# Up and down products as whole phases of 16 steps, attention half a period later, DMA transposes from unit 8 on

## The chip, the cores and the metric

The kernel runs on one core of one Trainium2 chip. The metric is the device time of the whole program in microseconds, lower is better. Most executions agree within about 0.3%. Twice in this study an execution ran far slower (519 us and 794 us); those are marked slow and no comparison uses them. Ratios are computed as the mean time of one kernel's fast runs over the mean of the other's fast runs of the same rounds, so they are not quite the ratio of the medians quoted beside them.

In this kernel PE does all matrix products, and its weight loads (PEld) run beside them; PE writes into banks of a memory called PSUM, from which ACT and DVE read. ACT does the gelu and copies finished rows out of PSUM, DVE does masks and scalings, POOL scales v and issues most loads, and SP issues DMA transposes and stores. The granted clock of a trace is the share of PE's full rate that the profile reports.

## The reference, cut to what matters

```python
# q, k, v: (8, 8, 576, 64) f32;  w_in: (512, 2048);  w_out: (2048, 512)
scores = q @ k.T / 8                        # per batch and head
ret    = scores * gamma_h ** (i - j) * (i >= j)
x      = (ret @ v) -> rows of (4608, 512)   # heads side by side
h      = x @ w_in
out    = (h * sigmoid(1.702 * h)) @ w_out
```

It is a decaying linear attention (a retention layer) followed by a two-layer network. The attention has little arithmetic; the two matrix products after it have most of it.

## The kernel before: the parts that matter

The 4608 rows are 36 units of 128 rows. Four units make a chunk of 512 rows, nine chunks in all. For each chunk, `up` is 16 steps of 4 matmuls (hidden block f, then gelu on ACT), `down` is 16 steps of 4 matmuls (row block r = i // 4). Each step is 4 matmuls of 512 columns.

```python
def up(c, f):
    bank = f"H{count['up'] % 2}"            # two PSUM banks, in turn
    ...                                     # 4 matmuls into bank
    op("act", ... gT[c % 2][:, f, :] <- gelu(bank))

def down(c, i, ybanks):
    r, s = divmod(i, 4)
    bank = ybanks[r % len(ybanks)]
    ...                                     # 4 matmuls; with s == 3 the bank is full:
    op("act", ... osb[u % 4] <- bank)       # four buffers for output rows
    op("sp",  ... out <- osb[u % 4])        # store, in SP's queue

def transpose_dma(u):                       # SP's queue too, waits for k and q of u
    op("sp", lambda e: e.dma_start_transpose(qkT[u % NQT].ap(), kq[sl]...), ...)

def block(m):                               # attention of units a = 2m, b = 2m + 1
    inter(a); inter(b)                      # state part, banks O0, O1
    scores(a + 2); scores(b + 2)            # of the next pair, banks S0/S1 and S2/S3
    scores_out(a + 2, 0)                    # DVE: mask, PSUM -> SBUF
    values(a); values(b)                    # PE, into O0, O1
    values_out(a); values_out(b)            # DVE: O0, O1 -> xT, the input of `up`
    ...                                     # DVE: rest of the masks
    if m > 4:
        ready_t(m + 3); fetch(m + 4, 2 * m + 6); ready_v(m + 2)
```

Every program order is fixed by hand: each engine has one in-order stream, and a small helper finds the semaphore waits. `fetch` issues loads on POOL's queue; its loads of v are made to wait until a given DMA transpose has landed.

The order of the products before, cut:

```python
play(16, lambda f: up(0, f), {...})                # chunk 0 up, units 4 to 6 between
...
play(8, lambda i: up_half(1, i, 1), {              # chunk 1 up, in two halves
    2: [lambda: head_in(8, "dve", "S2")],          # units 8, 9 transposed on PE
    4: [lambda: head_in(9, "dve", "S0")],
    6: [lambda: ready_v(4), lambda: scores_of(4)]})
play(16, lambda i: down(0, i, ("H0", "H1")), {..., 6: [lambda: block(4)], ...})
for m in range(5, NU // 2 + 1):                    # then half periods: downs of chunk c - 1
    ...                                            # alternate with ups of chunk c
    for x in "DDDDBDDUDDUUUUUUU" if m == 5 else "DDUDUDUDUDUDDUUU":
        ...                                        # D: down, banks S2 and S0;  U: up;  B: block
```

## Time and profile before

| | before |
|---|---|
| device time, median | 309.64 us (309.44 to 310.19, 6 runs) |
| span of the profiled run | 308.4 us |
| PE busy | 297.2 us (96%) |
| ACT, DVE, POOL busy | 121.3, 134.8, 113.0 us |
| PE idle between 60 and 80 us | 1.6 us |

Two rows of the profile page of the kernel before: part 1 gives busy time, share and instructions; in part 2 each digit is the busy share, in tenths, of one of 40 slices of the span.

```profile
PE 297.2 (96%) x2133; PEld 156.7 (51%) x2168; DVE 134.8 (44%) x279; ACT 121.3 (39%) x214; POOL 113.0 (37%) x139
PE   7799999999899999999999999999999999999996
```

PE is busy nearly throughout; the dips are the start, the end and the slice from 77 to 85 us. The view by windows, 60 to 80 us (window, length, busy time of PE, PEld, DVE, ACT and POOL, granted clock, DMA share, GB/s), has the 1.6 us of idle PE:

```profile
60.00:80.00 20.00, 18.40 (x155) 9.64 (x157) 11.31 (x22) 2.77 (x5) 9.91 (x12) 1.00 1.02 168
```

The Trainium skill ("Trainium Kernel Development and Optimization", section Performance Expectations) warns that matmul busy time is a bad measure of distance to the limit. The better reading here is the time from one matmul's start to the next, taken from the trace's records: 216 ns for 512 columns, 56 ns for 128. The kernel has 2168 matmuls (as many as the weight loads counted), the trace has 2133 records of them, so 35 are missing; a gap of exactly one more slot is a missing record and not a stall.

The timeline of PE in the kernel before (start, length, engine, line, operation, count) shows the first ten ups of chunk 0, one after the other:

```profile
19.38 8.81 PE L455 MATMUL psH<-xT,w_in_sb 128*128 128x512 bf16 x40
```

The next group starts at 28.02, so 40 matmuls took 8.64 us: 216 ns each, with gelu keeping up. The same timeline with all engines, between 58 and 79 us, holds the two places where PE waits for more than 0.5 us after the start (bracket: idle time before, and what ended it; SPq is SP's queue, and its length runs over merged issues, waits between them included):

```profile
58.74 15.87 SPq L339 DMA_TRANSPOSE qkT<-kq  x4
62.50 0.40 PE L415 MATMUL psS<-qkT 64*128 64x128 bf16 x8
63.39 0.40 PE L415 MATMUL psS<-qkT 64*128 64x128 bf16 x8 [0.49 <-DMA qkT<-kq]
...
74.67 1.54 SPq L500 DMA_DIRECT2D out_dram<-osb  x3
76.64 0.40 PE L415 MATMUL psS<-qkT 64*128 64x128 bf16 x8
77.12 0.60 ACT L494 ACTIVATE osb<-psS 128x512 f32<-128x512 f32 x1 [3.68 <-PE psS L415]
77.77 0.40 PE L415 MATMUL psS<-qkT 64*128 64x128 bf16 x8 [0.73 <-ACT osb L494]
```

At 63 us the scores of unit 11 wait for its DMA transpose. At 77 us the scores of unit 13 wait for ACT to empty the bank that the down product has just filled. By start-to-start times these two cost 0.68 and 0.92 us.

Two pieces of the chain of waits (start, length, what) say why the transpose at 63 us was late:

```profile
44.88 13.78 DMA kq<-in_q_dram
58.74 3.30 DMA qkT<-kq
```

A load of 128 KB took 13.8 us to land, in a backlog of weights and of v 8 to 11; its transpose then took 3.3 us.

### The profile page before, as it was taken

To read this page: it belongs to the slowest core of one execution; us is meant where nothing else is said; L and a number is where in the kernel's file an instruction comes from. 1 tells how busy PE (TensorE), PEld (TensorE's weight loads), DVE (VectorE), ACT (ScalarE), POOL (GpSimd) and SP (SyncE) were. 2 spreads that over 40 slices of the span, in tenths; PEclk is the share of its full clock that TensorE was granted. 3 is DMA by queue.
4 is the path that set the end of the run, shared out by engine and by line. 5 is a ranking of instruction groups with operands and counts; after the bars stand their busy time and mean duration, and the time that the engine had idled before them with its cause. 6 is when DMAs were issued, how large, how long until landed. Compare 5 with 4: busy or idle time off the path is not lost.

```text
span 308.4 us, 5131 instructions
## 1 busy us (share of the span) xinstructions
PE 297.2 (96%) x2133; PEld 156.7 (51%) x2168; DVE 134.8 (44%) x279; ACT 121.3 (39%) x214; POOL 113.0 (37%) x139
## 2 busy tenths in 40 slices
PE   7799999999899999999999999999999999999996
PEld 3444688544454545454545454545445454544444
DVE  5782863773764543545364725271717250100000
ACT  8566345211343333333333333334343424344411
POOL 9799991062462633614635606071000000000000
PEclk9999999999999999999999999999999999999999
DMA  9999999999999979999899999999610101010122
GB/s 141 194 207 189 189 205 184 138 132 165 175 215 125 166 164 153 192 177 144 202 144 194 159 124 155 134 143 123 61 66 5 52 19 36 34 60 31 45 53 85
DMA packets 116007, 39.93 MB, mean 129 GB/s; under 512 B 104912, under 2 KB 109264, under 8 KB 115984
## 3 DMA queue, kind: packets, MB, share of 16 engines
q0 software_dynamic: 80016, 22.55, 68.7%
q1 hardware_dynamic: 35968, 17.05, 23.8%
q8 instruction: 17, 0.28, 0.4%
q14 instruction: 6, 0.05, 0.0%
HBM read 36.70 MB, written 9.44 MB: 150 GB/s over the span
## 4 chain that ended last, share of the span: by engine, by line
PE 73%; POOL 13%; DMA 11%; issue 2%; SPq 0%; ACT 0%; DVE 0%; POOLq 0%; ACTq 0%
PE psS L486 32%; PE psH L455 31%; POOL kq L203 6%; DMA kq<-in_q_dram 6%; POOL vn L217 3%; PE psO L434 2%; DMA vn<-in_v_dram 2%; PE psS L415 2%; POOL vp L303 2%; PE psS L348 2%; PE psO L396 1%; PE psO L486 1%; DMA qkT<-kq 1%; POOL w_out_sb L232 1%; DMA out_dram<-osb 1%
## 5 line engine op out<-in xcount | busy, mean ns | idle before, releaser
L455 PE MATMUL psH<-xT,w_in_sb 128*128 128x512 bf16 x489 | 123.5, 379 | 2.4 <-issue 1.7
L460 ACT ACTIVATE gT<-psH 128x512 bf16<-128x512 f32 x128 | 76.4, 597 | 115.4 <-PE psH L455 115.4
L486 PE MATMUL psS<-w_out_sb,gT 128*128 128x512 bf16 x472 | 115.9, 379 | 0.5 <-issue 0.2
L455 PEld LDWEIGHTS psH<-xT,w_in_sb 128*128 128x128 bf16 x512 | 47.8, 98 | 58.4 <-ACT gT L460 3.5
L486 PEld LDWEIGHTS psS<-w_out_sb,gT 128*128 128x128 bf16 x480 | 46.1, 98 | 52.0
L217 POOL DMA_DIRECT2D vn<-in_v_dram x39 | 33.7, 882 | 93.3 <-DMA qkT<-kq 77.9
L424 DVE TENSOR_TENSOR pm<-psS,mask 128x512 bf16<-128x512 f32 x64 | 41.3, 683 | 41.1 <-PE psS L415 41.0
L203 POOL DMA_DIRECT2D kq<-in_q_dram x39 | 34.9, 904 | 0.0
L203 POOL DMA_DIRECT2D kq<-in_k_dram x39 | 34.8, 899 | 0.0
L494 ACT ACTIVATE osb<-psS 128x512 f32<-128x512 f32 x30 | 17.9, 597 | 32.9 <-PE psS L486 29.2
L444 DVE TENSOR_TENSOR xT<-psO,gq 128x512 bf16<-128x512 f32 x36 | 23.4, 684 | 13.9 <-PE psO L434 13.3
L378 DVE TENSOR_TENSOR kvf<-psS,kvf 64x256 f32<-64x256 f32 x24 | 10.1, 422 | 25.1 <-PE psS L348 24.8
L303 DVE TENSOR_TENSOR vp<-vn,vfac 128x512 bf16<-128x512 f32 x29 | 18.8, 684 | 1.4 <-DMA vn<-in_v_dram 1.3
L518 DVE COPY osb<-psS 128x256 f32<-128x256 f32 x1 | 0.4, 425 | 41.4 <-PE psS L512 41.4
L472 PE MATMUL psH<-xT,w_in_sb 128*128 128x256 bf16 x128 | 15.2, 273 | 0.0
L486 PE MATMUL psH<-w_out_sb,gT 128*128 128x512 bf16 x62 | 14.2, 379 | 0.2 <-issue 0.2
L415 PE MATMUL psS<-qkT 64*128 64x128 bf16 x288 | 12.3, 218 | 2.1 <-ACT qkT L331 0.9
L381 DVE CAST kv<-kvf 64x256 bf16<-64x256 f32 x36 | 13.3, 369 | 1.2
L477 ACT ACTIVATE gT<-psH 128x512 bf16<-128x512 f32 x16 | 9.6, 597 | 10.7 <-PE psH L472 10.7
L472 PEld LDWEIGHTS psH<-xT,w_in_sb 128*128 128x128 bf16 x128 | 12.0, 98 | 1.8 <-issue 0.2
L348 PEld LDWEIGHTS psS<-vp,kq 128*128 128x128 bf16 x128 | 9.2, 98 | 7.0 <-ACT kv L361 0.7
L348 PE MATMUL psS<-vp,kq 128*128 128x128 bf16 x128 | 12.4, 219 | 0.2 <-POOL vp L303 0.2
(62 smaller groups left out, 152.8 us busy)
## 6 DMA issues: line engine op xcount, KB each, us to landing
vn<-in_v_dram POOLq DMA_DIRECT2D x31, 256.0 KB, 5.0
out_dram<-osb SPq DMA_DIRECT2D x31, 256.0 KB, 2.4
kq<-in_k_dram POOLq DMA_DIRECT2D x31, 128.0 KB, 5.7
kq<-in_q_dram POOLq DMA_DIRECT2D x31, 128.0 KB, 5.8
w_in_sb<-in_moe_w_in_dram POOLq DMA_DIRECT2D x4, 512.0 KB, 10.0
w_out_sb<-in_moe_w_out_dram POOLq DMA_DIRECT2D x4, 512.0 KB, 14.4
out_dram<-osb SPq DMA_DIRECT2D x10, 128.0 KB, 2.3
vn<-in_v_dram POOLq DMA_DIRECT2D x8, 128.0 KB, 4.3
```

What stands on the lines that cost most here:

```text
L203: e.dma_start(kq[sl][p0 : p0 + n, i, :].rearrange("p (h d) -> p h d", d=DH), src[b, :, s0 : s0 + n, :].rearrange("h p d -> p h d"),)
L217: e.dma_start(vn[sl][p0 : p0 + n, :, :], v[b, :, s0 : s0 + n, :].rearrange("h p d -> p h d"),)
L303: op(eng, lambda e: e.tensor_tensor(vp[u % NVP].ap(), vn[sl].ap(), vfac[:, ty, :, None].to_broadcast([P, H, DH]), ALU.mult), reads=[f"vn{s ...
L348: op("pe", lambda e, hp=hp: e.matmul(kb[:, hp, :], kq[sl][:, 0, P * hp : P * hp + P], vp[u % NVP][:, 2 * hp : 2 * hp + 2, :], start=(first ...
L415: op("pe", lambda e, hp=hp, hh=hh, bank=bank: e.matmul(by_pair(bank)[:, hp, :], qt[64 * hh : 64 * hh + 64, hp, :], qt[64 * hh : 64 * hh + ...
L424: op("dve", lambda e: e.tensor_tensor(pm[u % 4][hh].ap(), by_pair(bank), m[:, None, :].to_broadcast([P, HP, P]), ALU.mult), reads=[bank, " ...
L444: op("dve", lambda e: e.tensor_tensor(xT[ch % 3][:, :, 128 * j : 128 * j + 128], by_pair(bank), gq[:, ty, :, :], ALU.mult), reads=[bank] + ...
L455: op("pe", lambda e, a=a: e.matmul(hb, w_in_sb[:, a, P * f : P * f + P], xT[c % 3][:, a, :], start=(a == 0), stop=(a == HP - 1)), reads=[f ...
L460: op("act", lambda e: e.activation(gT[c % 2][:, f, :], hb, AF.Gelu_apprx_sigmoid), reads=[bank], writes=[f"gT{c % 2}_{f}"])
L472: op("pe", lambda e, a=a, f=f, j=j: e.matmul(hb[:, j, :], w_in_sb[:, a, P * f : P * f + P], xT[c % 3][:, a, n], start=(a == 0), stop=(a == ...
L486: op("pe", lambda e, f=f: e.matmul(y, gT[c % 2][:, f, P * r : P * r + P], w_out_sb[:, f, :], start=(f == 0), stop=(f == NF - 1)), reads=[f ...
L494: op("act", lambda e: e.activation(osb[o].ap(), y, AF.Copy), reads=[bank], writes=[f"osb{o}"])
```

## The change

It aims at runs of one kind of product (16 ups, then 16 downs), with a paired attention block near the end of each run, and at having no PE transposes after unit 7. With ups and downs apart, both use banks H0/H1, and S0 to S3 belong to attention alone. The attention of a pair comes half a period later than before, so its transposes have longer. The diff, cut to its core:

```diff
         def head_vs(u):                     # values beside the next unit's scores
+            inter(u)
+            values(u)
+            values_out(u)
+            if u < 7:
+                head_s(u + 1)
             head_k(u, "dve")
 ...
-            if m > 4:
-                ready_t(m + 3)
-                fetch(m + 4, 2 * m + 6)
-                ready_v(m + 2)
+            if m + 2 < NU // 2:
+                ready_t(m + 2)
+                fetch((2 * m + 6, 2 * m + 7), (2 * m + 6, 2 * m + 7), 2 * m + 4)
 ...
+        scale_v(3, "pool")
         load_win(3)
-        scale_v(3, "pool")
 ...
-        for u in range(8, 12):
-            load_v(u)
-        load_kq(10)
-        load_kq(11)
 ...
+        ready_t(4)                          # units 8, 9 by DMA
+        fetch((8, 9), (10, 11), 8)          # these loads wait for the transpose of 8
 ...
-        play(8, lambda i: up_half(1, i, 1), {
-            2: [lambda: head_in(8, "dve", "S2")],
-            4: [lambda: head_in(9, "dve", "S0")],
-            6: [lambda: ready_v(4), lambda: scores_of(4)],
-        })
-        play(16, lambda i: down(0, i, ("H0", "H1")), {... 6: [lambda: block(4)], ...})
-        for m in range(5, NU // 2 + 1): ...  # "DDUDUDUDUDUDDUUU"
+        play(8, lambda i: up_half(1, i, 1), {})
+        steps = [(down, 0), (down, 1)]
+        for c in range(2, NCH):
+            steps += [(up, c), (down, c)]
+        events = {
+            (0, 2): [lambda: scores_of(4)],
+            (0, 5): [lambda: ready_t(5), lambda: fetch((10, 11, 12, 13), (12, 13), 10)],
+            (0, 7): [lambda: ready_v(4)],
+            (0, 9): [lambda: state(9)],
+        }
+        for m in range(4, NU // 2):
+            p = m - 4
+            events[p, 15 if m == 4 else 13] = [lambda m=m: block(m)]
+            ...                              # states at steps 4, 7; v scaled at 9
+        for p, (step, c) in enumerate(steps[:-1]):
+            ...                              # 16 steps of `step`, each followed by its events
```

`events[p, i]` runs after step i of phase p.

More of the change, by code (lines that the diff above doesn't have):

```diff
@@ L366, in state @@
         def state(u, bank="S1"):
+            if u >= NU or unit_info(u)[1] == 2:
+                return
             pb, kind, c = unit_info(u)
-            if kind == 2:
-                return
             kb = state_mm(u, bank, True)
@@ L553, in head_k, with head_vs, fetch @@
                 state(u, "S3")
-        def head_mid(u):
-            head_s(u)
-        def head_out(u):
-            head_v(u)
+        def head_vs(u):
+            inter(u)
[3 more added lines that the diff above has]
+                head_s(u + 1)
             head_k(u, "dve")
-        def fetch(m, held=None):
-            after = () if held is None else [f"qkT{held % NQT}q"]
-            for u in (2 * m, 2 * m + 1):
+        def fetch(vs, kqs, held):
+            for u in vs:
                 if u < NU:
-                    load_v(u, "pool", after)
-            for u in (2 * m, 2 * m + 1):
+                    load_v(u, "pool", [f"qkT{held % NQT}q"])
+            for u in kqs:
                 if u < NU:
@@ L605, in block @@
                 scores_out(b + 2, 1)
-            if m > 4:
-                ready_t(m + 3)
-                fetch(m + 4, 2 * m + 6)
-                ready_v(m + 2)
-        def states(m, i):
-            u = 2 * m + (i == 4)
-            if i in (1, 4) and u < NU:
-                state(u)
-        YB = ("S0", "S2")
+            if m + 2 < NU // 2:
+                ready_t(m + 2)
+                fetch((2 * m + 6, 2 * m + 7), (2 * m + 6, 2 * m + 7), 2 * m + 4)
         for i, src in enumerate((k, q)):
@@ L704, in bass_retnet_parallel__then__act_gelu_quick_kernel @@
             9: [lambda: head_in(4, "dve")],
-            11: [lambda: head_mid(4)],
+            11: [lambda: head_s(4)],
             12: [lambda: head_in(5, "dve")],
-            13: [lambda: head_out(4)],
-            14: [lambda: head_mid(5)],
-            15: [lambda: head_in(6, "dve"), lambda: head_out(5)],
+            13: [lambda: head_vs(4)],
+            14: [lambda: head_in(6, "dve")],
         })
-        head_mid(6)
+        head_vs(5)
         head_in(7, "dve")
         warm(1)
-        ready_t(5)
@@ L715, in bass_retnet_parallel__then__act_gelu_quick_kernel @@
-        fetch(6, 10)
-        ready_t(6)
+        ready_t(4)
+        fetch((8, 9), (10, 11), 8)
         play(8, lambda i: up_half(1, i, 0), {
-            1: [lambda: head_out(6)],
-            3: [lambda: head_mid(7)],
-            5: [lambda: head_out(7)],
-        })
-        play(8, lambda i: up_half(1, i, 1), {
-            2: [lambda: head_in(8, "dve", "S2")],
-            4: [lambda: head_in(9, "dve", "S0")],
-            6: [lambda: ready_v(4), lambda: scores_of(4)],
-        })
-        play(16, lambda i: down(0, i, ("H0", "H1")), {
-            1: [lambda: state(9)],
-            5: [lambda: ready_v(5)],
-            6: [lambda: block(4)],
-            9: [lambda: state(10), lambda: fetch(7, 12)],
-            11: [lambda: state(11)],
-            12: [lambda: ready_v(6)],
-            14: [lambda: ready_t(7), lambda: fetch(8, 14)],
-        })
@@ L736, in bass_retnet_parallel__then__act_gelu_quick_kernel @@
-        late = None
-        for m in range(5, NU // 2 + 1):
-            if 5 < m < NU // 2:
-                block(m)
-            if late is not None:
-                up(*late)
-            c, h = divmod(m - 1, 2)
-            iu = idn = 0
-            for x in "DDDDBDDUDDUUUUUUU" if m == 5 else "DDUDUDUDUDUDDUUU":
-                if x == "B":
-                    block(m)
-                    continue
-                if x == "D":
-                    down(c - 1, 8 * h + idn, ("S2", "S0") if m == 5 else YB)
-                    idn += 1
-                else:
-                    late = (c, 8 * h + iu)
-                    if iu < 7:
-                        up(*late)
-                    iu += 1
-                    states(m + 1, iu - 1)
@@ L757, in bass_retnet_parallel__then__act_gelu_quick_kernel @@
-        up(*late)
+            1: [lambda: head_vs(6)],
+            5: [lambda: head_vs(7)],
+        })
+        play(8, lambda i: up_half(1, i, 1), {})
[8 more added lines that the diff above has]
+        }
@@ new lines, in bass_retnet_parallel__then__act_gelu_quick_kernel @@
+        for m in range(4, NU // 2):
+            p = m - 4
+            events[p, 15 if m == 4 else 13] = [lambda m=m: block(m)]
+            events[p + 1, 3] = [lambda m=m: ready_v(m + 1)] if m == 4 else []
+            events[p + 1, 4] = [lambda m=m: state(2 * m + 2)]
+            events[p + 1, 7] = [lambda m=m: state(2 * m + 3)]
+            events[p + 1, 9] = [lambda m=m: ready_v(m + 2)]
+        for p, (step, c) in enumerate(steps[:-1]):
+            if step is up:
+                play(16, lambda i: up(c, i), {i: events.get((p, i), []) for i in range(16)})
+            else:
+                play(16, lambda i: down(c, i, ("H0", "H1")), {i: events.get((p, i), []) for i in range(16)})
```

## The prediction

> **What bounds the kernel now.** The tensor engine. The page has PE busy 297.2 of 308.4 us at full clock. The Trainium skill ("Trainium Kernel Development and Optimization", Performance Expectations) warns that matmul busy time is a bad measure, so I used the spacing of matmul starts in the timeline: 216 ns for 512 columns, 56 for 128, 28 for a paired scores or values matmul, and some 96 more at each switch between full-array, scores and values shapes. Over the program's order that is 295.4 us of issue. The rest: 1.2 us before the first matmul, 2.6 after the last, 7.3 of cold or waiting PE in the first 19.5 us, and three later stalls, together 1.7 us: 0.68 at 62.9 (scores of unit 11 wait for a DMA transpose), 0.12 at 69, 0.92 at 77 (scores of unit 13 wait for ACT to empty a bank shared with the down product). After 80 us I find no stall: interleaved up/down already runs at 216 ns per matmul.
>
> **What the change does.**
> 1. Separate phases: no arithmetic saved. The risk is ACT in a run of ups (gelu 0.60 us, starting 0.27 us after its product, two banks, 0.864 us per up), but ten consecutive ups at 19.4 us run at 216 ns already. Worth 0.
> 2. Units 8 and 9 by DMA transpose: 16 PE transposes of 56 ns go, 0.9 us, and two DVE copies of 0.69 us. The skill ("TensorE: Matmul & The Clock Gate", Part 4: PE-mode transpose) says that this path needs a DVE copy from PSUM; the trace agrees.
> 3. Values beside the next unit's scores: three fewer switches, 0.3 us.
> 4. Down on H0/H1, S0 to S3 for attention alone: the stalls of 0.92 and 0.12 us go.
> 5. Loads of v 8 to 11 and k/q 10, 11 move behind the transposes of 8, 9, out of a backlog (k/q 11 took 13.8 us to land, so units 10, 11 were transposed only at 58.7). The 0.68 us stall goes.
> 6. v3 scaled ahead of the last w_in issue: 0.25 us less wait at 18.2 us.
>
> **New waits.** Near 37 us DVE gets xT, two pm, two kv and the qkT copy in one burst (3.5 us against 3.3 of PE work): 0.4 us lost. Transposes of units 10 to 13 should land only about 1 us before blocks 4 and 5 need them: a 40% chance of losing 0.5 to 1.5 us, 0.4 on average. Later pairs have slack: a load-and-transpose round takes 13 us (transposes at 58.7, 71.7, 83.7, 96.5) of a 16 us period.
>
> **Sum.** 309.68 - 0.9 - 0.3 - 1.7 - 0.25 + 0.8 = 307.3 us. Nearly all of it is on the critical path, as PE is the path; it is just small. Range 306.2 to 308.9. Faster by over 2%: 0.02; that needs more than all stalls after 20 us. Within 2%: 0.97. Slower: 0.01.
>
> **What would show it.** PE busy falls by 1 us; starts stay 216 ns apart in runs of sixteen; scores no longer wait for ACT; the stretch from 60 to 80 us loses its 1.6 us of idle PE; units 8, 9 are transposed near 50 us. POOL's long wait for qkT stays and costs nothing.
>
> **What would make it wrong.** Runs of ups waiting for gelu (0.1 us each would cost over 10 us in 112 ups); xT late for a chunk's first up, as a block ends just two down steps (1.73 us) before it; transposes late for the blocks; or an early part that stalls more.

## The result and the profile after

The changed kernel takes 307.28 us (307.03 to 307.62, 6 runs), before 309.64 us; ratio 0.9922, interval 0.9909 to 0.9935. It is clearly faster, by 0.8%, and the predicted 307.3 us was met. Executions over 1.5% slower than the fastest of the same kernel are left out of the means.

The same two rows of the page of the changed kernel:

```profile
PE 299.5 (98%) x2152; PEld 149.7 (49%) x2152; DVE 131.7 (43%) x277; ACT 121.3 (40%) x214; POOL 113.0 (37%) x139
PE   8799999999999999999999999999999999999996
```

PE busy rose, although 16 matmuls are gone. This trace has all 2152 matmul records, where the one before lacks 35; busy time can't be compared across that. (Run b5 below has the PE program of the kernel before and all its 2168 records: there PE is busy 301.0 us, so against a complete trace busy time fell by 1.5 us.) What can be compared is a stretch with stalls in it: the eight in the eleventh slice is a nine now, and from 60 to 80 us PE is not idle at all:

```profile
60.00:80.00 20.00, 20.00 (x137) 9.97 (x136) 10.71 (x24) 2.99 (x5) 7.04 (x8) 1.00 1.24 183
```

The timeline of PE in the changed kernel, first phase:

```profile
53.86 2.75 PE L486 MATMUL psH<-w_out_sb,gT 128*128 128x512 bf16 x12
56.55 0.62 PE L415 MATMUL psS<-qkT 64*128 64x128 bf16 x16
57.10 6.22 PE L486 MATMUL psH<-w_out_sb,gT 128*128 128x512 bf16 x28
63.16 0.39 PE L348 MATMUL psS<-vp,kq 128*128 128x128 bf16 x4
63.38 5.34 PE L486 MATMUL psH<-w_out_sb,gT 128*128 128x512 bf16 x24
68.56 0.40 PE L403 MATMUL psO<-qkT,kv 128*128 128x64 bf16 x8
68.89 0.62 PE L415 MATMUL psS<-qkT 64*128 64x128 bf16 x16
```

No line has a bracket: neither the scores of 8 and 9 (at 56.55) nor those of 10 and 11 (68.89) wait. Over the whole trace, the only stalls left after 20 us are 0.06, 0.08 and 0.05 us, near 33 and 36 us, and 0.07 us at 46.9 us, which the kernel before has too.

From the summary of waits, longest first (engine, line, what it waited for: us in total, times, longest), one kind of wait of the weight loads. First the kernel before, then the changed one:

```profile
PEld psH L455 <- ACT gT L460: 3.5, 11, 0.3
```

```profile
PEld psH L455 <- ACT gT L460: 22.8, 72, 0.3
```

This looks like a new cost of 19 us, and is none: the matmuls of those ups still start 216 ns apart. An experiment below takes the wait away.

**The budget of the two profiled runs.** The spans differ by 3.07 us. Start-to-start times divide that: 16 transposes of 55.8 ns, 0.89 us; three fewer switches between matmul shapes at 96 ns, 0.29 us; the waits at 63, 69 and 77 us, 1.72 us less; new waits near 33 and 36 us, 0.19 us more; the first up starts 0.37 us earlier (19.00 against 19.38). Together 3.08 us. But the run ratio says 2.4 us (2.0 to 2.8 by its interval), not 3.07: the profiled run before took 310.16 us, 0.5 us above its kernel's median. Which of the terms was larger in that one run is settled below.

The 96 ns agree with the Trainium skill ("TensorEngine Tiling (Array Packing)", Key Properties), which says that changing the tiling mode drains the engine; it gives no time for it. Here a scores matmul (64 rows) after a full one costs 96 ns extra, and values (64 columns) after scores the same.

### The profile page after: what moved, and what is told of

It is laid out like the page before. It is cut to its first block, busy times and chain, and to the rows that moved or that the text cites. A ratio compares the mean times of both kernels' runs of the same rounds, so it can differ in the third digit from the quotient of the medians.

```text
span 305.3 us, 5121 instructions
## 1 busy us (share of the span) xinstructions
PE 299.5 (98%) x2152; PEld 149.7 (49%) x2152; DVE 131.7 (43%) x277; ACT 121.3 (40%) x214; POOL 113.0 (37%) x139
## 4 chain that ended last, share of the span: by engine, by line
PE 94%; POOL 3%; DMA 2%; issue 0%; ACT 0%; DVE 0%; POOLq 0%
PE psH L486 37%; PE psH L455 36%; PE psH L472 5%; PE psO L434 3%; PE psS L415 3%; PE psS L348 2%; DMA vn<-in_v_dram 2%; PE psS L486 2%; POOL kq L203 2%; PE psO L396 2%; PE psO L486 1%; PE psS L312 1%; PE psS L512 1%; PE psO L512 1%; POOL vp L303 0%
## 5 line engine op out<-in xcount | busy, mean ns | idle before, releaser
L455 PE MATMUL psH<-xT,w_in_sb 128*128 128x512 bf16 x512 | 115.5, 379 | 0.0
L486 PE MATMUL psH<-w_out_sb,gT 128*128 128x512 bf16 x512 | 115.3, 379 | 0.0
L486 PEld LDWEIGHTS psH<-w_out_sb,gT 128*128 128x128 bf16 x512 | 48.3, 98 | 56.4 <-ACT gT L460 1.9
L455 PEld LDWEIGHTS psH<-xT,w_in_sb 128*128 128x128 bf16 x512 | 42.4, 97 | 62.6 <-ACT gT L460 22.8
L494 ACT ACTIVATE osb<-psH 128x512 f32<-128x512 f32 x32 | 19.1, 597 | 106.7 <-PE psH L486 106.7
L303 DVE TENSOR_TENSOR vp<-vn,vfac 128x512 bf16<-128x512 f32 x29 | 18.8, 688 | 0.2
L472 PE MATMUL psH<-xT,w_in_sb 128*128 128x256 bf16 x128 | 14.5, 273 | 0.0
L376 DVE COPY kvf<-psS 64x256 f32<-64x256 f32 x12 | 5.1, 422 | 20.0 <-PE psS L348 19.9
L472 PEld LDWEIGHTS psH<-xT,w_in_sb 128*128 128x128 bf16 x128 | 11.8, 98 | 2.2 <-issue 0.2
L434 PE MATMUL psO<-pm,vp 128*64 128x128 bf16 x288 | 12.2, 223 | 0.5 <-DVE vp L303 0.5
```

What stands on the lines that cost most here:

```text
L434: op("pe", lambda e, hp=hp, hh=hh: e.matmul(ob[64 * hh : 64 * hh + 64, hp, :], vp[u % NVP][:, 2 * hp + hh, :], pm[u % 4][hh][:, hp, :], st ...
L455: op("pe", lambda e, a=a: e.matmul(hb, w_in_sb[:, a, P * f : P * f + P], xT[c % 3][:, a, :], start=(a == 0), stop=(a == HP - 1)), reads=[f ...
L472: op("pe", lambda e, a=a, f=f, j=j: e.matmul(hb[:, j, :], w_in_sb[:, a, P * f : P * f + P], xT[c % 3][:, a, n], start=(a == 0), stop=(a == ...
L486: op("pe", lambda e, f=f: e.matmul(y, gT[c % 2][:, f, P * r : P * r + P], w_out_sb[:, f, :], start=(f == 0), stop=(f == NF - 1)), reads=[f ...
L494: op("act", lambda e: e.activation(osb[o].ap(), y, AF.Copy), reads=[bank], writes=[f"osb{o}"])
```

## The experiments

Theory at the start, as in the prediction: PE is the path, so removed PE work and removed waits add up, and the phases themselves are worth nothing. Rival: the phases make the gain. The first four runs edit the kernel before; they shared the kernel-before runs on one chip (309.97 us median).

### b1_down_on_H: the wait at 77 us, by the bank

```diff
-  down(c - 1, 8 * h + idn, ("S2", "S0") if m == 5 else YB)
+  down(c - 1, 8 * h + idn, ("H0", "H1") if m == 5 else YB)
```

> The kernel before, with one edit: the second half of the first chunk's down product accumulates in banks H0/H1, not S2/S0, so that the scores of unit 13 share no bank with it. My theory (separate stalls add up): the 0.92 us wait of the scores for ACT near 77 us goes, and nothing else changes: about 308.7 us against 309.6, ratio 0.997. Rival (the phases of 16 steps made the gain, the bank did not): 309.6, ratio 1.000, or the wait moves elsewhere.

Measured: 310.37 us, ratio 1.0014 (1.0001 to 1.0027). A miss, with two lessons. The timeline of this run:

```profile
77.34 0.62 PE L415 MATMUL psS<-qkT 64*128 64x128 bf16 x16
77.50 0.60 ACT L494 ACTIVATE osb<-psH 128x512 f32<-128x512 f32 x1 [3.35 <-DMA out_dram<-osb]
...
83.64 1.04 PE L455 MATMUL psH<-xT,w_in_sb 128*128 128x512 bf16 x4 [0.69 <-ACT osb L494]
```

The scores no longer wait, but the second up after it now needs the bank that a down has just filled, and waits 0.85 us by start-to-start time: my edit moved the wait. The other line is more useful: ACT, which had nothing to do with a bank here, still started late, and waited for a *store*. In the kernel before the store of the first output rows was issued at 74.67 us, behind four transposes in SP's queue, landed at 77.04, and ACT started at 77.12. The scores waited for ACT, and ACT for the store that was to free `osb`.

### b2_kq_before_v: the wait at 63 us

```diff
-  for u in range(8, 12): load_v(u)
-  load_kq(10); load_kq(11)
+  load_v(8); load_v(9)
+  load_kq(10); load_kq(11)
+  load_v(10); load_v(11)
```

> The kernel before, with one edit: loads of k/q 10 and 11 go before those of v 10 and 11. My theory: the transposes of units 10, 11 start 1.5 to 2.5 us earlier, the 0.68 us wait of the scores of unit 11 near 63 us goes: about 309.0 us, ratio 0.998, and the 0.92 us wait near 77 stays or shrinks. Rival (the transposes are late for another cause, the transposing itself at 3.3 us): the wait stays, ratio 1.000.

Measured: 309.07 us, ratio 0.9976 (0.9964 to 0.9988), 0.7 us faster. In the trace the transposes start at 57.12 us and the scores of 10 and 11 run as one group of 16 at 63.59 without a wait. The wait at 77 us was only 0.10 us here. As expected: late loads caused the late transpose.

### b3_phases_only: runs of eight in place of alternation

```diff
-  for x in "DDDDBDDUDDUUUUUUU" if m == 5 else "DDUDUDUDUDUDDUUU":
+  for x in "DDDDBDDUDDUUUUUUU" if m == 5 else "DDDDDDDDUUUUUUUU":
```

> The kernel before, with one edit: from 95 us on each half period runs eight downs, then eight ups, in place of the alternation. My theory: alternation already runs at 216 ns per matmul, so nothing changes: ratio 1.000 within 0.001; starts of matmuls in the up runs stay 216 ns apart though the weight loads wait for gelu. Rival A (separate phases save PE time): ratio 0.993 or less. Rival B (runs of ups outrun gelu): over 0.05 us for each of 100 ups, so slower by 5 us or more.

Measured: 309.92 us, ratio 1.0004 (0.9988 to 1.0019). The order of ups and downs is worth nothing by itself: neither rival held. Its timeline has runs like this, 32 matmuls of 512 columns in 6.91 us to the next group's start, 216 ns each:

```profile
106.17 7.07 PE L486 MATMUL psS<-w_out_sb,gT 128*128 128x512 bf16 x32
113.08 1.89 PE L455 MATMUL psH<-xT,w_in_sb 128*128 128x512 bf16 x8
```

### b4_small_parts: everything but the phases

b1 and b2 together, the earlier scaling of v3, and units 8 and 9 by DMA:

```diff
+  ready_t(4)                                   # ahead of ready_t(5)
...
-  2: [lambda: head_in(8, "dve", "S2")],
-  4: [lambda: head_in(9, "dve", "S0")],
```

> The kernel before with all small parts and without the phases: down on H0/H1 near 70 us, k/q 10, 11 loaded before v 10, 11, units 8 and 9 transposed by DMA, v3 scaled before the last w_in issue; the alternation of ups and downs stays. My theory (the parts add up: 0.92 + 0.68 + 0.89 + 0.25 = 2.7 us): about 306.9 to 307.3 us, ratio 0.991 to 0.992, as the changed kernel. Rival (the phases carry the gain): at most half of it, 308.5 us or more.

Measured: 326.97 us, ratio 1.0556 (1.0533 to 1.058). 17 us *slower*; theory and rival both fell. The timeline shows where:

```profile
65.25 0.61 PE L415 MATMUL psS<-qkT 64*128 64x128 bf16 x8 [11.49 <-DMA qkT<-kq]
...
69.73 0.61 PE L415 MATMUL psS<-qkT 64*128 64x128 bf16 x8 [3.86 <-DMA qkT<-kq]
```

The scores of 8 and 9 wait for transposes that were issued at 50.1 and 52.5 us. From the view by tile, for transposes issued from 49 to 56 us: first the changed kernel, then this one.

```profile
DMA to landing us min/median/max: 3.1/3.2/3.3
```

```profile
DMA to landing us min/median/max: 15.1/16.2/17.2
```

The same two transposes, issued at almost the same time (50.0 and 51.6 us there), took five times as long. The difference lies in what is in flight: in the changed kernel no further load is issued between 38 us and the landing of the first of them, here nine loads are (v 8 to 11, k/q 10 and 11, the last at 46.8 us). This gave a new theory: **the parts are tied together.** Units 8 and 9 can only be transposed by DMA if the loads behind them are held back; then k/q 10 and 11 come later, so do their transposes, and the attention block has to come later too. c1 and c2 test both halves.

### a1_pe_transpose: units 8 and 9 on PE again, in the changed kernel

```diff
-  ready_t(4)
-  fetch((8, 9), (10, 11), 8)
...
-  play(8, lambda i: up_half(1, i, 1), {})
+  play(8, lambda i: up_half(1, i, 1), {
+      2: [lambda: head_in(8, "dve", "S2")],
+      4: [lambda: head_in(9, "dve", "S0"), lambda: fetch((8, 9), (10, 11), 8)]})
```

> The changed kernel, with units 8 and 9 transposed by PE again (in the second half of chunk 1's ups), the loads behind them released by the DVE copies. My theory: 16 more transposes of 56 ns and nothing else, 0.9 us more than the changed kernel (307.28): about 308.2 us, ratio to before 0.995. Rival (the DMA transposes gain by relieving DVE or cost by loading the DMA engines, so that the loss is over 1.5 us or under 0.3): 308.8 or more, or 307.5 or less.

Measured: 308.29 us, ratio 0.9958 (0.9944 to 0.9971), where the changed kernel has 0.9922: 1.1 us slower. Its trace has the 0.89 us of transposes and a wait of 0.25 us at 50 us for k/q 8, which have just landed there. As expected.

The Trainium skill ("TensorE: Matmul & The Clock Gate", Part 4: PE-mode transpose) gives about 275 ns for one transpose in a kernel. A transpose occupies 56 ns of PE's stream when others follow it; each has a duration of 219 ns in the trace. The saving follows the 56 ns.

### a2_third_bank and a6_third_bank_again: the weight loads' waits for gelu

```diff
-  bank = f"H{count['up'] % 2}"
+  bank = ("H0", "H1", "O0")[f % 3] if c > 1 and f < 12 else f"H{count['up'] % 2}"
```

> The changed kernel, with a third accumulator bank (O0) for the first twelve ups of each phase from chunk 2 on. The trace of the changed kernel has weight loads waiting 22.8 us in all for gelu, 72 times 0.3 us. My theory: these waits cost nothing, as the matmuls stay 216 ns apart: they go or shrink, and the time stays 307.3 (ratio to before 0.992, within 0.001). Rival (they cost time): up to 10 us faster.

Measured: 307.44 us median of five, ratio of the fast runs 0.9926 (0.9912 to 0.994), the same as the changed kernel. The profile fell in a slow execution (794 us), so it was run once more for a trace:

> The third-bank kernel once more, for a trace in the fast state (the earlier profile fell in a slow execution). Theory: the weight loads' waits for gelu in the up phases are gone or shrunk to the last four ups of a phase (from 22.8 us to under 8), the matmuls stay 216 ns apart, one time of about 307.4.

One run, 307.11 us, span 305.3 us, the same as that of the changed kernel. From its summary of waits:

```profile
PEld psH L455 <- ACT gT L460: 3.2, 10, 0.3
```

22.8 us of waits went down to 3.2 and the time did not move. A weight load that waits 0.3 us ahead of a matmul that isn't due yet costs nothing.

### a3_block_at_15 and a4_block_at_14: where the block stands in a phase

```diff
-  events[p, 15 if m == 4 else 13] = [lambda m=m: block(m)]
+  events[p, 15] = [lambda m=m: block(m)]                       # a3
+  events[p, 15 if m == 4 else 14] = [lambda m=m: block(m)]     # a4
```

> The changed kernel, with every attention block after step 15, the last of a phase, not after step 13. My theory: a chunk's first up then needs xT that DVE finishes about 1.2 us after the block's last matmul, so each of the seven chunks from 2 on waits 1.0 to 1.5 us: 8 us slower than the changed kernel, about 315. Rival (the place in the phase doesn't matter, as DVE is 43% busy): 307.3.

> The changed kernel, with every attention block after the first one after step 14, not 13. One down step (0.86 us) is left to hide DVE's 1.2 us: each of seven chunks waits 0.2 to 0.5 us, so 1.5 to 3.5 us slower than the changed kernel: 309 to 311. Rival (two steps of slack are not needed): 307.3.

Measured: a3 316.46 us, ratio 1.0219 (1.0205 to 1.0233); a4 310.15 us, ratio 1.0015 (1.0003 to 1.0028). Against 0.9922 for the changed kernel that is 9.2 and 2.9 us more. In both traces the first up of each of the seven chunks from 2 on waits for DVE's `xT`: 1.28 us each in a3 (1.26 the last), 0.38 us each in a4 (0.36), in sum 8.96 and 2.65 us. The first of them in a3, with the DVE line that ends it:

```profile
86.07 0.64 PE L434 MATMUL psO<-pm,vp 128*64 128x128 bf16 x16
86.56 1.28 DVE L444 TENSOR_TENSOR xT<-psO,gq 128x512 bf16<-128x512 f32 x2
...
87.89 4.28 PE L455 MATMUL psH<-xT,w_in_sb 128*128 128x512 bf16 x19 [1.19 <-DVE xT L444]
```

Each step of down between the block and the first up hides up to 0.864 us of that. With two steps (1.73 us) none of the 1.28 us is left.

### b5_stores_first: the wait at 77 us, by its new cause

```diff
-  ready_t(6)                                   # right behind ready_t(5)
...
-  9: [lambda: state(10), lambda: fetch(7, 12)],
+  9: [lambda: state(10), lambda: ready_t(6), lambda: fetch(7, 12)],
```

> The kernel before, with one edit: the transposes of units 12 and 13 are put behind the first output stores in SP's queue, not ahead of them. My new theory of the 0.92 us wait near 77 us: ACT waited there not for a bank but for the store of chunk 0's first rows, which sat in SP's queue behind transposes whose loads had not landed (store issued at 74.67, landed at 77.04, ACT started at 77.12). Then the store issues near 60 us, ACT starts at the end of its down product and the wait is 0.1 us or nothing: 0.1 to 0.8 us faster than before, ratio 0.9975 to 0.9997. My old theory (the scores share a bank with the down product): the wait stays 0.9 us, ratio 1.000.

Measured: 309.67 us, before 309.72 us, ratio 0.9995 (0.9981 to 1.0008). In the trace the first stores are issued at 61.78 us and the scores at 77 us wait 0.10 us. But they also waited just 0.10 us in b2 and b3, where the stores were still behind the transposes, and were issued at 73.13 and 73.74 us. So the wait of 0.92 us came about as b1 shows it, yet the store is only just too late or just in time: of the four traces with the stores behind the transposes it was too late in two, the profiled run before and b1 (issued at 74.67 and 74.96 us). These two executions took 310.16 and 310.83 us, above their medians of 309.64 and 310.37, and putting the stores first gained only 0.15 us by the ratio (interval -0.25 to 0.59). So the long wait seems to be the rarer case; how often it comes is not shown.

### c1_block4_at_6: the first block early, as before the change

```diff
-  (0, 7): [lambda: ready_v(4)],
+  (0, 4): [lambda: ready_v(4)],
+  (0, 15): [lambda: ready_t(6), lambda: fetch((14, 15), (14, 15), 12)],
...
-  events[p, 15 if m == 4 else 13] = [lambda m=m: block(m)]
+  events[p, 6 if m == 4 else 13] = [lambda m=m: block(m)]     # its own ready_t left out for m == 4
```

> The changed kernel, with the first attention block (units 8, 9, and the scores of 10, 11) after step 6 of chunk 0's down phase, where the kernel before has it, not after step 15. New theory (the parts are tied: transposing 8 and 9 by DMA pushes the loads of 10, 11 and so their transposes back, to landings of 65.5 and 67.6 us, and only the later block has room for that): the scores of units 10, 11 start near 61.2 us and wait 6 to 6.5 us: 313 to 314. Old theory (independent parts, the place of the first block is worth nothing): 307.3.

Measured: 315.53 us, ratio 1.0178 (1.0158 to 1.0199), 7.9 us slower than the changed kernel by the ratios. The timeline:

```profile
60.42 0.40 PE L403 MATMUL psO<-qkT,kv 128*128 128x64 bf16 x8
65.97 0.61 PE L415 MATMUL psS<-qkT 64*128 64x128 bf16 x8 [5.15 <-DMA qkT<-kq]
67.59 0.61 PE L415 MATMUL psS<-qkT 64*128 64x128 bf16 x8 [1.01 <-DMA qkT<-kq]
69.13 4.70 PE L486 MATMUL psH<-w_out_sb,gT 128*128 128x512 bf16 x12
```

By start-to-start times the waits are 5.22 and 1.29 us, as expected. The last line shows what I had left out: after the wait PE runs at half speed until about 73 us, with matmuls of 512 columns 427 ns apart; with the scores and values of the pair that adds about 2.7 us. The Trainium skill ("TensorE: Matmul & The Clock Gate", Part 1: the HAM clock gate) says that PE falls to half rate after an idle window of some 3.4 us and needs as long a busy one to recover; this trace agrees (5.2 us of idle; 216 ns return about 5.4 us after the second wait; an excess of 211 ns per matmul until then). Run c2 below agrees less well.

### c2_loads_not_held: the loads early, as before the change

```diff
+  for u in range(8, 12): load_v(u)            # early, behind scale_v(7)
+  load_kq(10); load_kq(11)
...
-  fetch((8, 9), (10, 11), 8)
...
-  (0, 5): [lambda: ready_t(5), lambda: fetch((10, 11, 12, 13), (12, 13), 10)],
+  (0, 5): [lambda: ready_t(5), lambda: fetch((12, 13), (12, 13), 10)],
```

> The changed kernel, with the loads of v 8 to 11 and k/q 10, 11 issued early, as in the kernel before, not held until the transposes of units 8 and 9 have landed. New theory (DMA transposes issued into a backlog of loads crawl, as in the run with all small parts, 15.1 us for unit 8 where the changed kernel has 3.3): the transposes of 8, 9 land near 65 and 69 us, their scores, due at 56.5, wait 9 to 13 us: 317 to 321. Rival (that run was slow through another of its edits or its alternation): 307.3 to 308.

Measured: 316.11 us, ratio 1.0204 (1.0185 to 1.0223), 8.7 us slower than the changed kernel by the ratios. The timeline and, from the view by tile, the landings of the transposes of 8 and 9:

```profile
60.47 0.60 PE L415 MATMUL psS<-qkT 64*128 64x128 bf16 x8 [3.01 <-DMA qkT<-kq]
64.11 0.61 PE L415 MATMUL psS<-qkT 64*128 64x128 bf16 x8 [3.05 <-DMA qkT<-kq]
```

```profile
DMA to landing us min/median/max: 9.8/10.7/11.5
```

The direction is as expected and the rival fell; the size was less than I expected (landings at 60.4 and 64.1 us, not 65 and 69; two waits of 3.1 and 3.3 us, and again PE at half speed). The half speed begins in the scores right after the first wait, where pairs of matmuls start 106 ns apart and not 56. So here 3.0 us of idle, less than the 3.4 us that the skill names, were enough. The loads suffer too: the last k/q load of this group took 17.3 us here, 13.3 to 13.8 us in the kernel before, where the transposes wait until these loads are through.

Why transposes and loads slow each other this much is open. The Trainium skill ("DMA: Bandwidth & Descriptors", Queues, rings and completion order) says that each DMA engine takes turns between its queues packet by packet. That alone would let me expect a transpose to take about twice its 3.3 us (an estimate: one turn in two), where the runs show 3 to 5 times.

## Why the prediction was right, and where it wasn't

**The time** was right: 307.3 predicted, 307.28 measured, and the class "within 2%".

**PE is the path; there is nothing to gain but its stalls and its small work:** right. After the change all stalls after 20 us sum to 0.26 us.

**Phases worth 0:** right for the order of ups and downs (b3, in runs of eight: 1.0004), and the wait for gelu is harmless (a6). It was wrong as a statement about the whole arrangement: the later place of the first block is worth 7.9 us (c1) once 8 and 9 go through DMA. I had treated the six points as independent and added them up. The sum held only because the change makes all of them at once; b4, which takes them without the later block and the held loads, is 17 us slower than before.

**Units 8 and 9 by DMA, 0.9 us:** right (a1: 1.1 us, of which 0.89 are transposes).

**Loads moved behind the transposes, 0.68 us:** right that this wait goes, and that its cause is the backlog (b2: 0.7 us). What I missed is that the move is a condition for point 2: with the loads in flight the transposes take 10 to 17 us, not 3.3 (c2, b4).

**The stall of 0.92 us at 77 us:** this term failed. Its cause isn't the shared bank alone but a store behind transposes in SP's queue (b1), and it was long in only two of four traces; in the other two (b2, b3) and in b5 the wait is 0.1 us. It was read from one profiled run that was slower than its kernel's median.

**New waits, 0.8 us:** too large. Near 33 and 36 us DVE's work cost 0.19 us, not 0.4, and the transposes of 10 to 13 were in time: those of 11 and 13 landed at 67.6 and 82.7 us, ahead of their scores, which begin right after those of 10 (68.89) and 12 (83.10). The margin of about 1 us was foreseen. This error and the last one, both about 0.6 to 0.8 us, cancelled: that the total came out to the decimal is luck.

**v3 scaled earlier, 0.25 us:** in the trace the wait of 0.26 us at 18.2 us is gone. The first up starts at 18.9 to 20.2 us in the traces of the kernel before and of its edited forms b1, b2, b3 and b5, and at 18.8 to 19.6 us in those of the changed kernel and its forms; that spread is larger than the effect, so its share of the time is not shown.

**"PE busy falls by 1 us":** the page shows a rise of 2.3 us, because the trace before lacks records. Against b5, whose trace is complete, busy time fell by 1.5 us (301.0 to 299.5), and a1, with the 16 transposes back, has 300.2: the direction was right.

With the stalls of b3 and b5 in place of those of the one slow profile, the sum closes: 0.89 transposes, 0.29 switches, 0.83 at 63 us (0.81 and 0.85; the two traces with the late store have 0.68 and 0.74), 0.17 at 69 us and 0.10 at 77 us (b5), less 0.19, is 2.09 us, and with the 0.25 us of v3, if it counts in full, 2.3 us; the ratio says 2.4 (2.0 to 2.8). The interval is too wide to settle single terms of 0.3 us.

## What to carry to other kernels

When one engine is the path, read its stalls by start-to-start times, and read them in more than one execution before pricing them: a wait that hangs on two DMAs arriving within a microsecond of each other is a draw and not a constant. Parts of a schedule change are seldom independent: ask of each part what it needs from the others (here a DMA transpose needed a quiet time on the DMA engines, the quiet time delayed the next loads, and the delay needed a later consumer), as a part taken alone can cost many times what the whole gains. A wait in the profile that ends before the next piece of work is due costs nothing, however long its sum.

## What the Trainium skill lacked or had wrong

- "DMA: Bandwidth & Descriptors", Rules for kernel authors: it says that a transpose next to ordinary DMAs needs nothing. That may hold for the data (all runs here were correct); for the time it doesn't: two transposes took 3.1 to 3.3 us on quiet DMA engines, 9.8 to 11.5 us (c2) and 15.1 to 17.2 us (b4) with a backlog of loads, and the loads slowed as well.
- "TensorEngine Tiling (Array Packing)": a change of tiling mode drains the engine, without a time; here about 96 ns each.
- "TensorE: Matmul & The Clock Gate", Part 4: about 275 ns per PE transpose in a kernel. That is a duration, which is 219 ns in the traces here; what a transpose costs in a stream isn't given, and here each transpose of 128x128 bf16 occupies PE for 56 ns.
- No page that I read has the executions at 519 us and 794 us of kernels that otherwise take 307 to 310 us (1 of 11 and 1 of 5 in two sets of runs here); in the profile of the one at 794 us matmuls of 512 columns were mostly 485 or 620 ns apart all through, though the clock was reported as 1.0 (as 0.56 for the one at 519 us, of which there is no trace).
